# A new written-out succession for a fused RWKV and MLP-mixer kernel, with other conditions for its first weights

## The chip, the cores and the metric

The kernel runs on one core of one Trainium2 chip. The metric is the device time of one execution in microseconds; of several executions the median counts. The engines are PE (TensorE), DVE (VectorE), ACT (ScalarE), POOL (GpSimd) and SP (SyncE, which here only issues transfers). Each engine works off its own list of instructions strictly in order and waits at the head of the list for semaphores.

## The reference

Inputs are r, k, v of shape (4, 8, 768, 48), per-head vectors w and u, and four weight matrices. First a linear attention with decay runs over 768 steps of time for each batch and head; then the heads are put side by side into x of shape (4, 768, 384), and one mixer block follows:

```python
for t in range(S):
    cur = einsum('bhd,bhe->bhde', u * k[t], v[t])
    y[t] = einsum('bhd,bhde->bhe', r[t], state + cur)
    state = w * state + einsum('bhd,bhe->bhde', k[t], v[t])

h  = maximum(x.T @ w_tok1, 0) @ w_tok2        # over the 768 steps of time, inner width 256
u  = x + h.T
h2 = maximum(u @ w_ch1, 0) @ w_ch2            # over the 384 channels, inner width 1536
return u + h2
```

## The kernel before

**Tiling.** The 768 steps of one batch are cut into 6 chunks of 128, which makes 24 units (batch, chunk), all heads of a unit at once. A unit's k, r and v are three loads of 128 x 384 f32 (192 KB each) into pools of 8 buffers per kind.

**Attention of a unit u** is a fixed set of named steps: `kp`, `rp` scale k and r by powers of the decay (DVE or POOL), `trk`, `trr` transpose them on the PE (units 14 to 23 by a DMA transpose `i:t` instead), `rk` (or `rkk` and `rkr`) bring the result to SBUF (ACT), `at` makes the scores on the PE, `AT0`, `AT1` mask them (DVE, some after a copy `raw` on ACT), `vb` casts v (ACT), `kv` and `S` carry the state, `pr`, `pg`, `adg`, `yd` make the diagonal term, `yS` and `y` sum the output in PSUM, and `x` writes the unit's part of x. `yi` of unit 3 adds the diagonal term on the PE by an f32 matmul.

**Mixer of a batch.** `hid` multiplies the six chunks of x by w_tok1 (into `h1_ps`), `hr` is the relu, `bk` and `us` (or `ux` and `ub` for half of batch 0) make u, `tu` and `uT` turn it, `z` multiplies by w_ch1, `zr` is the relu, `h` multiplies by w_ch2, `os` adds, `i:o` stores. There are 24 `z` steps of three matmuls each in a batch, and 24 `h` steps of twelve matmuls in four parts.

**Weights.** They come by six transfers that POOL issues (`i:w0` w_tok1, `i:w1` w_tok2, `i:w2` and `i:w4` the halves of w_ch1, `i:w3` and `i:w5` the halves of w_ch2); these cast f32 to bf16. `hid` needs w0, `ub` and `bk` need w1, `z` needs w2 and later w4, `h` needs w3 and later w5. POOL works them off between its products.

**What sets the order.** `ORDER` (line 508) names for each engine the succession of its steps. A planner (`Plan.run`, line 70) replays these lists with assumed costs, from the settings in `CFG` (line 444); the sequence of start times that comes out of it is the sequence in which the steps are emitted. Its assumed times set three things in the program beside that: how many filler matmuls (`Plan.fill`, line 142) stand in gaps of the PE, which shared product of POOL or DVE waits for which (`products_in_turn`, line 158), and the turn in which pooled buffers are handed out. The engine's own order is that of `ORDER`.

In `CFG`, `wafter` gives for each weight a step that the planner lets its request wait for (`x:r4` is the landing of unit 4's r); it enters `graph` alone (line 426), and `weight` (line 753) issues a DMA with no condition beyond its place on POOL. `slack` lengthens the assumed landing of a load, `half` is the time up to which the planner takes the PE to be slow, and `y_m` lists the units whose output `y` has a PSUM bank of its own from the common pool of four in place of the fixed bank.

One condition is made in the program too: `hold` (line 495) keeps the load of a unit's k back until a step is done. `hold={6: ('y', 5), ...}` holds `i:k6` until the last matmul of `y5`, and with it everything behind `i:k6` on SP:

```python
if i in CFG.get("hold", {}) and nm == "k":
    first = INS["".join(map(str, CFG["hold"][i]))]
    tc.add_manual_dep(ins.ins, first.ins.name, ..., reason="weights first")
```

SP issues loads, stores and DMA transposes. The program has eight semaphores for them in turn, so a transfer is issued only when the eighth before it has landed.

PSUM has four banks in a common pool (`psM`) and four with fixed use (`psA`).

Of the kernel before, what the change touches and what calls it, by code (L numbers as in the profile page):

```python
# [180 lines left out]
def graph(do, cfg):  # L181
# [256 lines left out]
    for s in p.steps:  # L438
# [42 lines left out]
    wafter={0: 'x:r4', 1: 'kp5', 2: 'rp5', 4: 'rp5', 3: 'rp5', 5: 'rp5'},  # L481
    slack={'v5': 0.9},
# [16 lines left out]
    y_m=(2, 4),  # L499
    apart=2.0,  # L500
    half=8.3,
# [28 lines left out]
    ),  # L530
    "DVE": (
# [11 lines left out]
    ),  # L543
    "ACT": (
# [558 lines left out]
```

## Time and profile before

| | |
|---|---|
| median of 3 runs | 166.47 us (165.52 to 167.43) |
| the profiled execution, its own time | 165.6 us |
| its span, first to last instruction | 163.9 us |
| mean granted TensorE clock | 0.984 |
| PE busy | 154.8 us |
| DVE, ACT, POOL busy | 119.7, 74.0, 59.1 us |
| read from and written to HBM | 20.65 and 4.72 MB |

All durations below are of the one profiled execution. It was faster than the median of the runs by 0.9 us. A row of the timeline has the start in us, the length in us, the engine, the line, the operation and what it writes and reads; since a helper records every instruction, all have the line L617, and rows are told apart by engine and tile. "SPq" is the issue of a transfer by SP. A row of the windows has the stretch, its length, and for each engine the busy time with the count of instructions; then the granted clock of the PE, the busy share of the DMA engines and GB/s.

### The profile page before, as it was taken

How to read it: one execution, taken by the hardware profiler on the slowest of the kernel's cores; microseconds unless marked ns; L12 is line 12 of the kernel's file. 1: busy time of each engine (PE TensorE's matmuls, PEld its weight loads, DVE VectorE, ACT ScalarE, POOL GpSimd, SP SyncE). 2: the span in 40 equal slices, each digit the busy share in tenths (PEclk: the TensorE clock that was granted, in tenths of full speed). 3: DMA queues.
4: the chain of work that ended last, by engine and by line, in shares of the span. 5: the costliest groups of instructions: out<-in, count | busy, mean ns of one | idle time of the engine just before them, and what ended most of it. 6: DMA issues, size and time to landing. Idle time of an engine off the chain costs nothing.

```text
span 163.9 us, 3809 instructions
## 1 busy us (share of the span) xinstructions
PE 154.8 (94%) x1487; PEld 99.2 (61%) x1487; DVE 119.7 (73%) x254; ACT 74.0 (45%) x160; POOL 59.1 (36%) x74
## 2 busy tenths in 40 slices
PE   6988799999999999999999999999999999999990
PEld 3476565656576767665666565666566666655670
DVE  5679878547089998896998989999999665223330
ACT  4899671552389635588504420445134102621400
POOL 7157860000055495954459542182702000000000
PEclk9999789999999999999999999999999999999997
DMA  5999999999999998999499999999934032501212
GB/s 106 222 212 219 152 201 201 185 184 198 199 221 237 210 233 168 214 159 208 99 167 206 226 212 150 236 234 151 204 67 145 0 72 43 177 0 48 96 48 98
DMA packets 97427, 26.26 MB, mean 160 GB/s; under 512 B 90753, under 2 KB 97410, under 8 KB 97410
## 3 DMA queue, kind: packets, MB, share of 16 engines
q1 hardware_dynamic: 93920, 22.88, 69.9%
q0 software_dynamic: 3488, 3.15, 12.1%
q8 instruction: 11, 0.18, 0.4%
q14 instruction: 6, 0.05, 0.1%
q10 hardware_dynamic: 2, 0.00, 0.0%
HBM read 20.65 MB, written 4.72 MB: 155 GB/s over the span
## 4 chain that ended last, share of the span: by engine, by line
PE 84%; SPq 7%; DMA 3%; ACT 3%; issue 1%; DVE 0%; ACTq 0%
PE h_ps L617 34%; PE z_ps L617 29%; SPq L617 7%; PE y_ps L617 6%; PE at_ps L617 5%; PE hT_ps L617 4%; DMA ld_v<-in_v_dram 3%; PE tr_ps L617 3%; PE kv_ps L617 3%; ACT rk L617 1%; PE t_ps L617 1%; ACT raw L617 0%; ACT vb L617 0%; PE ut_ps L617 0%; ACT S L617 0%
## 5 line engine op out<-in xcount | busy, mean ns | idle before, releaser
L617 PE MATMUL h_ps<-wch,zr 128*128 128x384 bf16 (+1 forms) x300 | 55.2, 320 | 0.0
L617 PE MATMUL z_ps<-uT,wch 128*128 128x384 bf16 x288 | 53.9, 326 | 0.1
L617 ACT ACTIVATE zr<-z_ps 128x384 bf16<-128x384 f32 x66 | 30.8, 492 | 50.7 <-PE z_ps L617 50.2
L617 PEld LDWEIGHTS <-zr 128*128 128x128 bf16 x300 | 27.4, 98 | 15.2
L617 PEld LDWEIGHTS <-wch 128*128 128x128 bf16 x288 | 26.6, 98 | 16.2 <-issue 0.2
L617 DVE TENSOR_TENSOR AT<-at_ps,mask 128x512 bf16<-128x512 f32 x43 | 28.9, 684 | 1.5 <-PE at_ps L617 1.2
L617 DVE TENSOR_SCALAR zr<-z_ps 128x384 bf16<-128x384 f32 x30 | 15.9, 553 | 11.7 <-PE z_ps L617 11.2
L617 POOL TENSOR_TENSOR kpr<-ld_r,wp 128x384 bf16<-128x384 f32 x14 | 14.6, 1044 | 24.9 <-DVE pr L617 22.2
L617 POOL TENSOR_TENSOR kpr<-ld_k,wn 128x384 bf16<-128x384 f32 x16 | 16.3, 1019 | 10.0 <-DMA ld_k<-in_k_dram 5.8
L617 DVE TENSOR_TENSOR osb<-u_sb,h_ps 128x384 f32<-128x384 bf16 (+1 forms) x22 | 11.7, 532 | 11.0 <-PE h_ps L617 11.0
L617 ACT COPY rk<-tr_ps 128x512 bf16<-128x512 bf16 (+1 forms) x23 | 15.1, 682 | 8.9 <-PE tr_ps L617 8.8
L617 PEld LDWEIGHTS <-rk 48*128 48x128 bf16 (+1 forms) x272 | 11.0, 97 | 8.7 <-issue 4.6
L617 PEld LDWEIGHTS <-kpr 128*128 128x128 bf16 x192 | 12.5, 101 | 5.2 <-issue 1.6
L617 POOL TENSOR_TENSOR yd<-vb,adg 128x384 f32<-128x384 bf16 x12 | 10.3, 858 | 12.0 <-ACT vb L617 8.3
L617 DVE TENSOR_TENSOR x_b<-y_ps,yd 128x384 bf16<-128x384 f32 x23 | 12.6, 552 | 2.1 <-PE y_ps L617 1.9
L617 ACT CAST vb<-ld_v 128x384 bf16<-128x384 f32 x24 | 12.2, 514 | 3.4 <-DMA ld_v<-in_v_dram 3.3
L617 DVE TENSOR_TENSOR u_sb<-x_b,hT_ps 128x384 bf16<-128x384 bf16 x21 | 11.2, 549 | 2.3 <-PE hT_ps L617 1.9
L617 PE MATMUL tr_ps<-ident,kpr 128*128 128x128 bf16 x112 | 10.7, 233 | 1.0 <-ACT rk L617 0.6
L617 PEld LDWEIGHTS <-wtok 128*128 128x128 bf16 x90 | 8.1, 97 | 4.8 <-issue 0.4
L617 PE MATMUL at_ps<-rk 48*128 48x128 bf16 x192 | 9.8, 222 | 1.2 <-ACT rk L617 0.4
L617 DVE TENSOR_TENSOR pr<-tr_ps,rk 128x512 bf16<-128x512 bf16 x14 | 5.9, 419 | 5.9 <-ACT rk L617 5.8
L617 PE MATMUL h_ps<-x_b,wtok 128*128 128x384 bf16 x48 | 10.0, 325 | 0.0
(87 smaller groups left out, 157.5 us busy)
## 6 DMA issues: line engine op xcount, KB each, us to landing
ld_k<-in_k_dram SPq DMA_DIRECT2D x24, 192.0 KB, 3.8
ld_r<-in_r_dram SPq DMA_DIRECT2D x24, 192.0 KB, 3.9
ld_v<-in_v_dram SPq DMA_DIRECT2D x24, 192.0 KB, 3.8
out_dram<-osb SPq DMA_DIRECT2D x23, 192.0 KB, 2.3
wch<-in_moe_w_ch_dram POOLq DMA_DIRECT2D x4, 576.0 KB, 12.2
wtok<-in_moe_w_tok_dram POOLq DMA_DIRECT2D x2, 384.0 KB, 5.4
u_bc<-in_u_dram SPq DMA_DIRECT2D x1, 192.0 KB, 4.4
out_dram<-osb SPq DMA_DIRECT2D x2, 96.0 KB, 2.6
```

Source lines behind the costliest of these rows:

```text
L617: ins = tc.keep_in_program_order(f(*args, **kw))
```

## The change

Four settings of the planner are changed, and the succession of all five engines is written anew. The first weight's request waits in the plan for the landing of v of unit 4 in place of r of unit 4, the second and third for the landing of r of unit 5 in place of the products `kp5` and `rp5`. The assumed extra time of v5 goes from 0.9 to 0.6, the slow time of the PE from 8.3 to 9.0, and the units with an output bank of their own are 1, 3 and 5 in place of 2 and 4. `hold` stays as it was.

Only the heads of the lists are shown, up to about the first channel matmul of batch 0; behind that the steps of a list are the same but stand in another order, and some 60 steps go from one engine to another (21 `zr` from ACT to DVE and 19 the other way, some of `kp`, `rp`, `yd`, `ku`, `rku` between DVE and POOL).

```diff
-    wafter={0: 'x:r4', 1: 'kp5', 2: 'rp5', 4: 'rp5', 3: 'rp5', 5: 'rp5'},
-    slack={'v5': 0.9},
+    wafter={0: 'x:v4', 1: 'x:r5', 2: 'x:r5', 4: 'rp5', 3: 'rp5', 5: 'rp5'},
+    slack={'v5': 0.6},
...
-    y_m=(2, 4),
+    y_m=(1, 3, 5),
     apart=2.0,
-    half=8.3,
+    half=9.0,
...
     "PE": (
-        "trk0 trr0 trk1 at0 wu trr1 trk2 trr2 pg0 at1 y0 kv0 pg1 at2 pg2 kv1 trk3 trr3 yS1 yS2 y1 kv2 trk4 at3 pg3 trr4 kv3 y2 trk5 at4 yS3 "
-        "trr5 yi3 y3 kv4 pg4 at5 yS5 pg5 ux0_0_1 yS4 hid0_bank0 y4 y5 hid0_bank1 hid0_0 hid0_1 hid0_2 hid0_3 hid0_4 hid0_5 ux0_0_2 ux0_0_0 "
-        "ub0_0_0 bk0_3 ub0_0_2 bk0_5 ub0_0_1 bk0_4 tu0_3 tu0_5 z0_0_0 z0_0_4 tu0_4 z0_0_3 z0_0_2 z0_0_5 z0_1_0 z0_0_1 z0_0_9 z0_1_1 z0_1_2 "
+        "trk0 trr0 wu kv0 at0 trk1 pg0 trr1 trk2 trk3 y0 trr2 at1 yS1 kv1 pg1 trr3 at2 pg2 yS2 kv2 y1 trk4 y2 trr4 at3 trk5 pg3 kv3 yS3 at4 "
+        "trr5 yi3 y3 at5 yS4 pg5 y4 pg4 hid0_bank0 hid0_bank1 kv4 hid0_0 hid0_1 hid0_2 yS5 y5 hid0_3 ux0_0_2 hid0_4 hid0_5 ux0_0_0 ux0_0_1 "
+        "ub0_0_0 bk0_4 bk0_3 ub0_0_2 ub0_0_1 bk0_5 tu0_3 tu0_4 z0_0_0 tu0_5 z0_0_3 z0_0_4 z0_1_0 z0_1_1 z0_1_2 z0_0_1 z0_0_5 z0_0_2 z0_0_7 "
...
     "DVE": (
-        "kp1 kp0 rp0 rp2 rp1 pr0 AT0_0 uw AT1_0 pr1 yd0 AT0_1 x0 pr2 AT1_1 AT1_2 yd1 AT0_2 x1 pr3 AT0_3 S2 yd2 AT1_3 pr4 yd3 AT1_4 AT0_4 x2 "
-        "pr5 AT0_5 AT1_5 yd5 yd4 x4 x5 hr0_0a hr0_1b uT0_0_0 us0_3 us0_5 us0_4 uT0_5 uT0_3 zr0_0_3 zr0_0_9 zr0_0_4 zr0_0_11 zr0_1_1 "
+        "kp0 rp0 kp2 uw pr0 AT0_0 rp1 AT1_0 rp2 yd0 rp3 x0 pr1 AT0_1 yd1 pr2 AT0_2 AT1_1 AT1_2 S2 x1 yd2 pr3 AT1_3 AT0_3 x2 yd3 AT0_4 AT1_4 "
+        "pr4 pr5 AT0_5 AT1_5 yd4 yd5 x4 x5 hr0_0a hr0_1b us0_4 us0_3 uT0_0_0 us0_5 uT0_5 zr0_0_4 zr0_1_0 zr0_0_3 zr0_1_2 zr0_0_5 zr0_1_3 "
...
     "ACT": (
-        "lnw wn0 wn1 wp0 wp2 wn2 wp1 rkk0 rkr0 vb0 raw0 rkk1 rkr1 rkk2 rkr2 raw1 vb1 S0 vb2 S1 rk3 wGm vb3 rk4 S3 vb4 rk5 x3 S4 raw5 vb5 "
+        "lnw wn0 wn2 wp0 wp1 vb0 wn1 rkk0 rkr0 wp2 S0 raw0 rkk1 rkr1 vb1 rkk2 raw1 rkr2 wGm S1 vb2 rk3 rk4 vb3 vb4 rk5 S3 x3 raw5 vb5 S4 "
...
     "POOL": (
-        "kp2 kp3 rp3 kp4 rp4 i:w0 kp5 rp5 i:w1 i:w2 i:w4 i:w3 i:w5 rp8 kp8 kp9 kp10 yd7 yd8 rp11 yd9 rp12 kp12 yd10 yd11 rp13 kp13 yd12 "
+        "kp1 kp3 kp4 rp4 i:w0 kp5 rp5 i:w1 i:w2 i:w4 i:w3 i:w5 kp7 rp9 rp7 kp8 yd6 kp9 rp10 kp11 yd8 rp11 yd10 rp12 rp13 yd11 kp13 yd12 "
...
     "SP": (
-        "i:k1 i:r2 i:k0 i:r0 i:r1 i:v0 i:k2 i:v1 i:k3 i:r3 i:v2 i:k4 i:r4 i:k5 i:v3 i:r5 i:v4 i:v5 i:k6 i:r6 i:k7 i:r7 i:v6 i:r8 i:k8 i:v7 "
+        "i:k0 i:r0 i:v0 i:k2 i:k1 i:r1 i:k3 i:v1 i:r2 i:r3 i:v2 i:k4 i:v4 i:r4 i:k5 i:v3 i:r5 i:v5 i:k7 i:k6 i:r6 i:v6 i:r9 i:r7 i:r8 i:k8 "
...
```

More of the change, by code (lines that the diff above doesn't have):

```diff
@@ L509 @@
     "PE": (
[20 rows of a table removed]
[20 rows of a table added]
     ),
     "DVE": (
[11 rows of a table removed]
[11 rows of a table added]
     ),
     "ACT": (
[8 rows of a table removed]
[8 rows of a table added]
     ),
     "POOL": (
-        "kp2 kp3 rp3 kp4 rp4 i:w0 kp5 rp5 i:w1 i:w2 i:w4 i:w3 i:w5 rp8 kp8 kp9 kp10 yd7 yd8 rp11 yd9 rp12 kp12 yd10 yd11 rp13 kp13 yd12 "
-        "kp14 rp14 rp16 ku14 ku15 ku16 kp16 yd14 rku16 yd16 ku18 rku18 yd15 kp19 rp18 kp18 rp19 yd17 rku19 kp20 rp21 rku20 rp22 kp21 yd19 "
-        "kp23 ku23 rku22 rp23 yd23 "
[3 rows of a table added]
     ),
     "SP": (
[5 rows of a table removed]
[5 rows of a table added]
         "i:o3_3 i:o3_4 i:o3_5a i:o3_5b "
```

76 rows, old and new, of the table ORDER are left out of this document.

## The prediction

> **What bounds the kernel now.** I read the page's shares and its chain first, then the windows by stage, then the rows of the stage that the change moves.
>
> ```profile
> span 163.9 us, 3809 instructions
> PE 154.8 (94%) x1487; PEld 99.2 (61%) x1487; DVE 119.7 (73%) x254; ACT 74.0 (45%) x160; POOL 59.1 (36%) x74
> PE 84%; SPq 7%; DMA 3%; ACT 3%; issue 1%; DVE 0%; ACTq 0%
> ```
>
> TensorE (PE) is busy 94% of the span and holds 84% of the chain that ended last; the other shares of the chain lie at its start. The windows cut the span at the first matmul of the token mixing of batch 0 (24.64) and at the first matmul of its channel mixing (29.88); the last rows are shorter stretches.
>
> ```profile
> core 0: us, PE busy (x) PEld busy (x) DVE busy (x) ACT busy (x) POOL busy (x), PEclk, DMA share, GB/s
> 0.00:24.64 24.64, 20.23 (x253) 13.87 (x254) 18.41 (x50) 19.04 (x39) 15.70 (x29) 0.93 1.02 185
> 24.64:29.88 5.24, 5.19 (x44) 3.12 (x40) 4.38 (x10) 1.51 (x4) 0.00 (x0) 1.00 1.15 199
> 29.88:160.30 130.42, 129.40 (x1197) 82.19 (x1196) 96.90 (x196) 53.42 (x117) 43.45 (x45) 1.00 0.79 156
> 10.00:15.00 5.00, 4.31 (x89) 3.63 (x87) 4.73 (x14) 4.87 (x13) 3.35 (x5) 1.00 1.08 207
> 15.00:20.00 5.00, 3.67 (x65) 2.52 (x62) 4.43 (x10) 3.83 (x9) 4.43 (x5) 0.87 1.01 167
> 18.69:22.10 3.41, 3.29 (x32) 2.10 (x29) 2.98 (x6) 2.32 (x5) 3.41 (x5) 0.50 1.31 197
> 65.00:70.00 5.00, 4.60 (x58) 3.10 (x57) 4.57 (x11) 2.57 (x6) 5.00 (x7) 1.00 0.99 199
> ```
>
> From 29.88 on the PE is idle 130.42 - 129.40 = 1.02 us in all. The work behind that point is the same in both kernels (the two successions hold the same steps behind `z0_0_0`, but that `tu0_5` takes the place of `tu0_4`), so no succession can win more than 1.0 us there. The rest of what can be won lies ahead of 29.88: 24.64 - 20.23 = 4.4 us of idle PE, and a stretch of 3.41 us at half clock (0.50).
>
> What lets the first channel matmul go are two things: units 0 to 5 must be through attention, and the first part of `wch1` must have landed. The weights are asked for by POOL between its products:
>
> ```profile
> 14.90 1.00 POOL L617 TENSOR_TENSOR kpr<-ld_r,wp 128x384 bf16<-128x384 f32 x1
> 15.85 0.89 POOL L617 DMA_DIRECT2D wtok<-in_moe_w_tok_dram  x1
> 16.76 1.01 POOL L617 TENSOR_TENSOR kpr<-ld_k,wn 128x384 bf16<-128x384 f32 x1
> 18.32 0.99 POOL L617 TENSOR_TENSOR kpr<-ld_r,wp 128x384 bf16<-128x384 f32 x1 [0.55 <-DMA ld_r<-in_r_dram]
> 19.25 0.77 POOL L617 DMA_DIRECT2D wtok<-in_moe_w_tok_dram  x1
> 20.02 3.19 POOL L617 DMA_DIRECT2D wch<-in_moe_w_ch_dram  x4
> DMA to landing us min/median/max: 8.3/12.2/17.0
> ```
>
> The last line is from the view of the tile `wch`: the earliest of its four transfers took 8.3 us, so `w2` landed at about 20.02 + 8.3 = 28.3, 1.6 us before its first reader at 29.88. The six weights keep the DMA engines full from about 18 us to the last landing: the last of the four issues began near 20.02 + 3.19 - 0.8 = 22.4, and 22.4 + 17.0 = 39.4.
>
> **The change part by part.** *The weights' conditions (`wafter`).* They enter only the planner's graph; `weight()` issues a bare DMA. In POOL's written-out order `i:w0` stands behind `rp4` and `i:w1` behind `rp5` in both kernels, so in the program nothing is asked for earlier: the issue still hangs on r4 and r5. These edits cost and win nothing by themselves. The same holds for `slack` and `half`, beyond the filler matmuls (27 before, 28 now, 14 of them now in one place, behind `pg0`); they lie in gaps, so nothing for them.
>
> *The loads' order.* r4 goes from place 13 to 14 of SP's list, r5 from 16 to 17, v4 comes four places earlier. A load of 192 KB at the 207 GB/s of the 10 to 15 us row takes 0.95 us. So `rp4` moves from 14.90 to 15.85 at the latest, `w0` from 15.85 to 16.8, and `rp5`, which waited for its load until 18.32, to 19.3; `w1` and `w2` are asked for behind it, at 20.2 and 21.0.
>
> *A load slips past the hold.* SP was held at `i:k6` until the last matmul of `y5` (`hold={6: ...}`), which kept all later loads behind the weights' requests:
>
> ```profile
> 14.67 2.78 SPq L617 DMA_DIRECT2D ld_v<-in_v_dram  x2
> 24.83 0.37 SPq L617 DMA_DIRECT2D ld_k<-in_k_dram  x1
> 25.24 0.60 SPq L617 DMA_DIRECT2D ld_r<-in_r_dram  x1
> ```
>
> Now `i:k7` stands ahead of `i:k6`, and the hold is on k6 alone; k7 takes the eighth buffer and waits for nothing but old landings. Its 192 KB follow v5 at once, into the time when the weights move. What that costs can be read where both queues were busy (30 to 36 us, the second pair) and where the weights were alone (22 to 28 us, the first line), in the views of the DMA queues:
>
> ```profile
> q0 software_dynamic: 782, 1.15, 112.9%
> ...
> q0 software_dynamic: 1161, 0.89, 93.7%
> q1 hardware_dynamic: 1161, 0.22, 33.5%
> ```
>
> Alone the weights (q0) moved 1.15 MB in 6 us, 0.192 MB/us; beside loads (q1) 0.89 MB, 0.148 MB/us, while the loads got 0.037 MB/us, packet for packet the same count. k7's 0.197 MB beside weights would take 5.3 us and cost them 5.3 x 0.044 / 0.192 = 1.2 us. The other end is nothing: between 15 and 20 us the engines moved 167 GB/s against 207, a hole of 0.2 MB, as large as k7. I take 1.2, since the load comes last on SP, behind the hole. The Trainium skill, "DMA: Bandwidth & Descriptors", section "Queues, rings and completion order", has each engine take turns between queue rows packet by packet; the equal counts of 1161 agree, and the sum would be the same by it. The later requests of `w0` to `w2` cost little beside that, because the queue in front of them is then emptier by the same loads. So `w2` lands at 28.3 + 1.2 = 29.5 (28.3 to 30.4 with both in full).
>
> *Attention of unit 5.* Its chain ends in these rows, all at or just behind the half clock:
>
> ```profile
> 19.86 0.63 PE L617 MATMUL tr_ps<-ident,kpr 128*128 128x128 bf16 x4
> 20.28 1.59 PE L617 MATMUL y_ps<-yd,ident_w 128*128 128x384 f32 x2
> 22.02 0.37 PE L617 MATMUL kv_ps<-vb,kpr 128*128 128x96 bf16 x4
> 22.22 0.24 PE L617 MATMUL g_ps<-UW,pr 128*128 128x2 bf16 x4
> 22.39 0.40 PE L617 MATMUL at_ps<-rk 48*128 48x128 bf16 x8
> ...
> 22.61 0.64 ACT L617 CAST S<-kv_ps 48x192 bf16<-48x192 f32 x2
> 23.27 0.58 ACT L617 CAST raw<-at_ps 128x512 bf16<-128x512 f32 x1
> ...
> 23.88 0.43 DVE L617 TENSOR_TENSOR AT<-raw,mask_b 128x512 bf16<-128x512 bf16 x1 [0.36 <-ACT raw L617]
> 24.30 1.02 DVE L617 TENSOR_TENSOR yd<-vb,g_ps 128x384 f32<-128x384 bf16 x2
> 25.42 1.02 DVE L617 TENSOR_TENSOR x_b<-y_ps,yd 128x384 bf16<-128x384 f32 x2
> ...
> 29.88 1.14 PE L617 MATMUL z_ps<-uT,wch 128*128 128x384 bf16 x6
> ```
>
> `rp5` ended at 19.3 and its transpose began at 19.86, 0.55 us of slack; one slot later (0.95) leaves 0.4 us of delay for `trr5` and `yi3`. Behind `y3` the new succession has `at5` at once, with `kv4` and `pg4` behind it: they started 0.37 us ahead of it (22.02 to 22.39), so `at5` stays at about 22.4. ACT then does `raw5` ahead of `S4` (0.64), which lets it start at about 22.9, right behind `at5`, not at 23.27; DVE's masking follows at 23.5 for 23.88, and from there the list is the same length: two `yd`, two `x`. Three of the six token steps run before `y5` now; DVE's two `x` still gate the last two, so they hide no more. The attention thus lets the channel mixing go 0.0 to 0.4 us earlier, I take 0.2: 29.7. It ends last, `w2` (29.5) just before it. Term one: 29.7 - 29.88 = **-0.2 us**, from -1.3 (k7 in the hole, r5 on time) to +0.6 (`w2` at 30.4).
>
> *The rest of the succession.* From 29.88 some 60 steps change engines, about as many from DVE to ACT or POOL as back, and nearly all change place. No trace shows the new waits. The lower bound is all idle gone, -1.0. For the upper bound, in the list of waits of this stretch stands
>
> ```profile
> PE tr_ps L617 <- ACT rk L617: 0.6, 2, 0.4
> ```
>
> a mean of 0.3 us; the worst 5 us (65 to 70) have 0.40 idle. If ten of the 18 later units got such a wait, it would be +3.0. I take a doubling of today's idle, **+1.0 us**, nearest to the row of 1.02: each engine works strictly in its list, and a list fitted to assumed landings meets others.
>
> The sum against the profiled execution's own 165.6 (span 163.9 and 1.7 around it): 165.6 - 0.2 + 1.0 = 166.4. The median of the runs, 166.47, is 0.9 above that execution, so the forecast for a median is **167.3 us**.
>
> **The rivals.** *The weights come on time and the attention earlier* (faster): k7 fills the 0.2 MB hole, r5 is not late, and the channel mixing starts at 28.4, right behind `w2`: -1.5; half of the 1.0 idle goes: -0.5; 164.5 on the median. For it speaks the hole; against it that r5 stands a place later.
>
> *The late list* (slower): POOL and DVE lists of units 6 to 9 meet landings in another order than assumed, because k7 is there early and the weights, then k6 and r6, late. POOL has `rp9` ahead of `rp7` and `kp8`, at 1.0 us each, and `trk8` waits for `kp8`; a single late load holds the products behind it and, over the transposes, the PE. It decides once the loads behind the weights come over 0.5 us later than now; price ten waits of 0.3 us instead of the one us taken: +2.0, 169.3. Against it: today's list had to meet late landings too.
>
> *The half clock falls on full work* (slower). The stretch 18.69 to 22.10 follows a thin window (3.67 busy of 5.00). The new list has a thin place too, `trk5` waiting for `kp5`. Should the stretch come after 24.64, 1.7 us of matmul work is lost where no idle hides it: 169.0. Conversely the Trainium skill, "TensorE: Matmul & The Clock Gate", section "Why this matters for your kernels", says that only idle gaps of about 3 us throw the clock back. Such a kernel would have no half-clock stretch: the attention would be up to 1.7 us earlier, but `w2` at 29.5 holds the first channel matmul, so 167.1. The trace speaks against that rule: the 0.50 came with no PE gap that long, the whole idle of 15 to 20 us being 1.33.
>
> *It does nothing of what it says*: requests unmoved, the orders worth the same, 166.5.
>
> **How the numbers follow.** Chances: forecast 0.38, on-time 0.20, late list 0.20, half clock on full work 0.12, nothing 0.06, no half clock 0.04. One per cent of 166.47 is 1.7 us, about what a measurement of this kernel can tell from no change (three runs spread from 165.5 to 167.4). Faster (under 164.8) holds nearly all of the on-time case, 0.19; slower (over 168.1) the late list, nearly all of the half clock, and 0.05 of the forecast's spread, 0.35; within 1%: 0.46. The range, 164.4 to 169.6, reaches from the on-time case to just beyond the late list; what is left out is a half-clock stretch and a late list together, or all idle gone.
>
> **What would show it.** Right: k7's load issued right behind v5, before 20 us; `wch`'s shortest transfer longer than 8.3 us or asked for near 21; first `z_ps` between 29.4 and 30.2; PE idle behind it about 2 us. Wrong: a first `z_ps` before 29.0, PE idle over 3 or under 0.5 us behind it, or a row of clock under 1.00 after 24.64. If the r5 slot is not late at all, the load term has failed.

## The result

The changed kernel is slower: 167.86 us, the median of 4 executions (167.62 to 168.1), against 166.0 of the kernel before, measured beside it (4 executions, 165.03 to 167.43; the three of the first table are among them). These medians differ by 1.1%; the recorded ratio, which isn't simply that of the medians, is 1.0147, with a 95% interval from 1.0101 to 1.0193. The range that was forecast holds the time, and 167.3 lies 0.6 us below it. The class that had been given most (within 1%) holds the time against the 166.47 us that it was reckoned from, but not the ratio.

The ratios leave out executions that lie over 1.5% above the fastest of their kernel; of the kernel before these are 10 of 25, 4 of 13 and 16 of 34 on the three chips of the experiments, and with them its medians there would be 166.04, 166.59 and 166.49 in place of 165.75, 166.07 and 165.83, so that a ratio near 1.006 is hardly a difference.

The profiled execution took 167.8 us. From the page of the changed kernel, the span, the shares of the engines and the shares of the chain that ended last:

```profile
span 165.7 us, 3812 instructions
PE 156.0 (94%) x1488; PEld 100.5 (61%) x1488; DVE 119.7 (72%) x249; ACT 73.1 (44%) x160; POOL 64.4 (39%) x79
PE 76%; DVE 8%; SPq 7%; DMA 3%; POOL 2%; ACT 2%; issue 1%; POOLq 0%; DVEq 0%
```

The PE's share of the chain fell from 84% to 76%, and DVE and POOL came into it with 8% and 2%. Ahead of the first channel matmul lie 2.6 us of POOL's links and 3.4 of DVE's, where the kernel before has none of either; another 9 us of DVE's lie behind it. To see which of the two parts is longer I cut both spans at the first channel matmul and at the end of the last matmul. First the windows of the kernel before (columns as in the prediction), then those of the changed one:

```profile
15.00:16.00 1.00, 0.88 (x26) 0.71 (x22) 1.00 (x3) 0.91 (x3) 1.00 (x2) 1.00 1.16 232
16.00:17.00 1.00, 0.67 (x16) 0.33 (x8) 1.00 (x3) 0.64 (x2) 0.98 (x2) 1.00 0.64 121
29.88:159.92 130.04, 129.40 (x1197) 82.19 (x1196) 96.56 (x195) 53.42 (x117) 43.45 (x45) 1.00 0.79 156
159.92:163.90 3.98, 0.00 (x0) 0.00 (x0) 0.35 (x1) 0.00 (x0) 0.00 (x0) 0.77 0.30 98
```

```profile
15.00:16.00 1.00, 0.68 (x10) 0.48 (x11) 1.00 (x4) 0.95 (x3) 0.10 (x1) 1.00 0.40 74
17.43:24.26 6.83, 5.77 (x56) 3.88 (x58) 5.27 (x11) 3.49 (x7) 6.62 (x9) 0.50 1.18 188
31.34:162.35 131.01, 130.02 (x1197) 83.07 (x1197) 95.33 (x189) 52.38 (x117) 48.60 (x50) 1.00 0.78 154
162.35:165.70 3.35, 0.00 (x0) 0.00 (x0) 0.35 (x1) 0.00 (x0) 0.00 (x0) 1.00 0.27 87
```

The first channel matmul comes at 31.34 in place of 29.88 (+1.46), the stretch from it to the last matmul takes 131.01 in place of 130.04 (+0.97), and what follows the last matmul 3.35 in place of 3.98 (-0.63). Together +1.80, the difference of the spans. Around the span lie 2.1 us in place of 1.7.

How the start became late is read from the chain that ended last. Some of its links between 12 and 20 us, first of the kernel before, then of the changed one (start, length, what):

```profile
12.83 4.69 DMA ld_v<-in_v_dram
```

```profile
12.29 4.37 DMA ld_r<-in_r_dram
...
17.66 0.90 POOL wtok L617
18.58 1.02 POOL kpr L617
```

Before, the chain ran over the landing of v3; now it runs over the landing of r4 and from there along POOL. POOL's timeline in the changed kernel:

```profile
16.72 1.00 POOL L617 TENSOR_TENSOR kpr<-ld_r,wp 128x384 bf16<-128x384 f32 x1 [1.62 <-DMA ld_r<-in_r_dram]
17.66 0.90 POOL L617 DMA_DIRECT2D wtok<-in_moe_w_tok_dram  x1
18.58 1.01 POOL L617 TENSOR_TENSOR kpr<-ld_k,wn 128x384 bf16<-128x384 f32 x1
19.78 1.00 POOL L617 TENSOR_TENSOR kpr<-ld_r,wp 128x384 bf16<-128x384 f32 x1 [0.19 <-DMA ld_r<-in_r_dram]
...
21.49 3.19 POOL L617 DMA_DIRECT2D wch<-in_moe_w_ch_dram  x4
24.67 1.04 POOL L617 TENSOR_TENSOR kpr<-ld_k,wn 128x384 bf16<-128x384 f32 x1
```

`rp4` begins at 16.72 in place of 14.90 and waited 1.62 us for its load. Behind it on POOL follow at once the request of w0 (0.90 us of POOL's own time) and `kp5`, whose own load k5 had landed at 17.40: it was the queue that held it until 18.58. `rp5` is 1.46 us later than before for two reasons that nearly coincide: the queue was done with `kp5` at 19.59, and r5 itself landed late, so that `rp5` waited 0.19 us more for it.

r4 was late mainly because it was asked for late. Its issue on SP, before and in the changed kernel:

```profile
10.76 1.23 SPq L617 DMA_DIRECT2D ld_r<-in_r_dram  x1
```

```profile
12.29 0.81 SPq L617 DMA_DIRECT2D ld_r<-in_r_dram  x1
```

Of these 1.53 us, 0.52 had arisen by the issue of k4 (10.51 in place of 9.99; the loads of units 0 to 3 stand in another order too), and 0.99 is the issue of v4, which now stands between k4 and r4. The transfer itself took 4.4 us in place of 4.0. The hole at 15 to 16 us, in which the DMA engines moved 74 GB/s where the kernel before had 232 in the same microsecond, falls on it and can have cost this difference.

The PE takes this up twice, and the half clock falls on what follows (PE timeline of the changed kernel):

```profile
17.77 0.61 PE L617 MATMUL tr_ps<-ident,kpr 128*128 128x128 bf16 x4 [0.63 <-POOL kpr L617]
...
19.64 0.61 PE L617 MATMUL tr_ps<-ident,kpr 128*128 128x128 bf16 x4 [0.72 <-POOL kpr L617]
...
21.79 0.61 PE L617 MATMUL tr_ps<-ident,kpr 128*128 128x128 bf16 x4
...
24.14 0.43 PE L617 MATMUL at_ps<-rk 48*128 48x128 bf16 x8
...
31.34 0.65 PE L617 MATMUL z_ps<-uT,wch 128*128 128x384 bf16 x3
```

`trr4` waited 0.63 us for `rp4`, with `at3` behind it in the list, and `trk5` 0.72 us for `kp5`. `trr5` then began at 21.79, 1.01 us after the end of `rp5` (20.78): by then it was the PE, at half clock from 17.43 to 24.26 and without a gap from 19.64 on, that was late. `at5` came at 24.14 in place of 22.39, and the first channel matmul 1.46 late.

Two more lines of the changed kernel, the issue of k7 on SP and the landings of the tile `wch`:

```profile
17.61 0.91 SPq L617 DMA_DIRECT2D ld_k<-in_k_dram  x1
```

```profile
DMA to landing us min/median/max: 8.3/12.0/16.9
```

k7 slipped past SP's hold, as forecast, and `w2` landed at 21.49 + 8.3 = 29.8, 1.5 us before its reader: the weights did not hold the first channel matmul.

### The profile page after: what moved, and what is told of

It is laid out like the page before. It is cut to its first block, busy times and chain, and to the rows that moved or that the text cites. A ratio compares the mean times of both kernels' runs of the same rounds, so it can differ in the third digit from the quotient of the medians.

```text
span 165.7 us, 3812 instructions
## 1 busy us (share of the span) xinstructions
PE 156.0 (94%) x1488; PEld 100.5 (61%) x1488; DVE 119.7 (72%) x249; ACT 73.1 (44%) x160; POOL 64.4 (39%) x79
## 4 chain that ended last, share of the span: by engine, by line
PE 76%; DVE 8%; SPq 7%; DMA 3%; POOL 2%; ACT 2%; issue 1%; POOLq 0%; DVEq 0%
PE h_ps L617 30%; PE z_ps L617 27%; SPq L617 7%; PE hT_ps L617 4%; PE y_ps L617 4%; PE at_ps L617 4%; DMA ld_r<-in_r_dram 3%; PE kv_ps L617 2%; DVE AT L617 2%; PE tr_ps L617 2%; DVE x_b L617 2%; DVE yd L617 1%; POOL kpr L617 1%; ACT rk L617 1%; DVE S L617 1%
## 5 line engine op out<-in xcount | busy, mean ns | idle before, releaser
L617 PE MATMUL h_ps<-wch,zr 128*128 128x384 bf16 (+1 forms) x300 | 54.4, 320 | 0.0
L617 ACT ACTIVATE zr<-z_ps 128x384 bf16<-128x384 f32 x64 | 29.3, 490 | 54.0 <-PE z_ps L617 53.9
L617 PE MATMUL z_ps<-uT,wch 128*128 128x384 bf16 x288 | 52.8, 326 | 0.0
L617 DVE TENSOR_SCALAR zr<-z_ps 128x384 bf16<-128x384 f32 x32 | 16.9, 553 | 11.8 <-PE z_ps L617 10.8
L617 POOL TENSOR_TENSOR kpr<-ld_r,wp 128x384 bf16<-128x384 f32 x15 | 15.4, 1033 | 25.0 <-DMA ld_r<-in_r_dram 20.3
L617 POOL TENSOR_TENSOR kpr<-ld_k,wn 128x384 bf16<-128x384 f32 x15 | 15.5, 1034 | 12.3 <-DMA ld_k<-in_k_dram 8.3
L617 POOL TENSOR_TENSOR yd<-vb,adg 128x384 f32<-128x384 bf16 x13 | 11.1, 853 | 22.3 <-DVE adg L617 17.3
L617 DVE TENSOR_TENSOR u_sb<-x_b,hT_ps 128x384 bf16<-128x384 bf16 x21 | 10.7, 549 | 5.4 <-PE hT_ps L617 5.4
L617 PE MATMUL h_ps<-x_b,wtok 128*128 128x384 bf16 x48 | 10.5, 326 | 0.1
L617 PE MATMUL hT_ps<-h1r,wtok 128*128 128x384 bf16 x42 | 9.3, 326 | 0.2 <-ACT h1r L617 0.2
```

Of the source, the lines that this page charges most:

```text
L617: ins = tc.keep_in_program_order(f(*args, **kw))
```

## The experiments

Every kernel was measured beside the kernel before, on the same chip. The medians are of the executions that the ratio of each uses; the other columns are from the one profiled execution, "rest" being the stretch from the first channel matmul (first z) to the end of the last matmul.

| kernel | median (n) | ratio and interval | rp5 | first z | rest | behind it |
|---|---|---|---|---|---|---|
| before | 165.75, 166.07, 165.83 (15, 9, 18) | 1 | 18.32 | 29.88 | 130.04 | 3.98 |
| after | 167.86 (4) | 1.0147 [1.0101, 1.0193] | 19.78 | 31.34 | 131.01 | 3.35 |
| x1 | 167.62 (3) | 1.0107 [1.0041, 1.0172] | 18.40 | 30.11 | 132.01 | 3.38 |
| x2 | 167.65 (9) | 1.0116 [1.0074, 1.0157] | 19.84 | 31.79 | 130.83 | 3.58 |
| x3 | 166.83 (7) | 1.0059 [1.0004, 1.0114] | 18.42 | 32.02 | 130.69 | 3.79 |
| x7 | 165.48 (9) | 0.9999 [0.9952, 1.0046] | 19.13 | 31.07 | 130.82 | 4.01 |
| x4 | 168.61 (4) | 1.0151 [1.0089, 1.0212] | 20.31 | 32.03 | 132.02 | 3.35 |
| x5 | 168.1 (4) | 1.0117 [1.0061, 1.0173] | 20.13 | 31.75 | 131.31 | 3.34 |
| x6 | 166.57 (9) | 1.0039 [0.9992, 1.0086] | 19.02 | 30.16 | 131.00 | 3.34 |
| x9 | 167.9 (4) | 1.0110 [1.0054, 1.0166] | 20.00 | 31.57 | 131.01 | 3.32 |
| y1 | 167.66 (9) | 1.0083 [1.0051, 1.0116] | 19.69 | 31.25 | 130.99 | 3.36 |
| y2 | 166.92 (9) | 1.0062 [1.0022, 1.0102] | 18.16 | 30.76 | 131.99 | 3.35 |
| y3 | 166.97 (11) | 1.0067 [1.0024, 1.0110] | 19.19 | 30.15 | 131.03 | 3.92 |
| y4 | 167.32 (10) | 1.0114 [1.0068, 1.0159] | 18.59 | 30.16 | 130.99 | 3.35 |

The profiled executions of x3, x7 and y2 were 1.2 to 2.1 us above their medians and that of x4 0.8, while that of y4 was 0.8 below, so their first z is not typical.

### The start and the rest, each alone (x1, x2)

x1 has the start of the kernel before (units 0 to 5, loads, weights, token mixing of batch 0) and the changed succession behind it; the settings and the heads of the other three lists go back as well. Against the changed kernel, on POOL and SP:

```diff
-        "kp1 kp3 kp4 rp4 i:w0 kp5 rp5 i:w1 i:w2 i:w4 i:w3 i:w5 kp7 rp9 rp7 kp8 ...
+        "kp2 kp3 rp3 kp4 rp4 i:w0 kp5 rp5 i:w1 i:w2 i:w4 i:w3 i:w5 kp7 rp9 rp7 kp8 ...
-        "i:k0 i:r0 ... i:k4 i:v4 i:r4 i:k5 i:v3 i:r5 i:v5 i:k7 i:k6 i:r6 ...
+        "i:k1 i:r2 ... i:k4 i:r4 i:k5 i:v3 i:r5 i:v4 i:v5 i:k6 i:k7 i:r6 ...
```

> The start of the kernel before (all steps of units 0 to 5, the loads and weights, the token mixing of batch 0) with the succession of the changed kernel behind it; k7's load stands behind the held k6. In the changed kernel the first channel matmul came 1.46 us later than before and the stretch from there to the last matmul was 0.97 us longer (131.06 against 130.09). If these two are separate: first z_ps at 29.9 within 0.4, stretch 131.0, time 0.6 to 1.0 above the kernel before. Rival, that the longer stretch only echoes the late start (loads and weights coming late into units 6 to 9): stretch 130.1, time as before within 0.3.

Measured: 1.0107, with the first channel matmul as early as before (30.11) but a rest of 132.01. The windows, the PE's waits behind 30 us and the timeline of POOL, all of x1:

```profile
30.11:162.12 132.01, 130.16 (x1200) 83.18 (x1197) 94.97 (x188) 52.43 (x116) 49.99 (x51) 1.00 0.77 154
```

```profile
PE tr_ps L617 <- ACT rk L617: 0.7, 1, 0.7
PE tr_ps L617 <- POOL kpr L617: 0.3, 1, 0.3
PE kv_ps L617 <- DVE S L617: 0.3, 1, 0.3
PE t_ps L617 <- DVE u_sb L617: 0.3, 1, 0.3
```

```profile
39.82 0.99 POOL L617 TENSOR_TENSOR kpr<-ld_k,wn 128x384 bf16<-128x384 f32 x1 [16.52 <-DMA ld_k<-in_k_dram]
```

The last line is `kp7`, the first product behind the weights in the changed POOL list, with `rp9`, `rp7` and `kp8` queued behind it. With k7 behind the held k6 it ran at 39.82; in the changed kernel, where k7 slips past, it ran at 24.67. So x1 does not hold the rest as the changed kernel has it. The table sorts by this: the changed succession with k7 early takes 130.99 to 131.01 behind the first channel matmul in five kernels, and 131.31 in x5; with k7 held 131.99 to 132.02 in three (x1, x4, y2). The early k7 is worth 1.0 us there. And the same 131.0 stands in x6 with an early first z (30.16) as in the changed kernel with a late one: a rest that is only an echo of the late start is ruled out.

x2 is the other half: the changed start, k7 ahead of k6 included, and the succession of before behind it (in the two lists of the diff above, the changed line up to `i:w5` and up to `i:k6`, and then the steps of before).

> The start of the changed kernel (with k7's load ahead of the hold) and the succession of the kernel before behind it. Separate parts: first z_ps at 31.3 within 0.4, stretch 130.1, time 1.0 to 1.6 above the kernel before. Rival, echo: stretch 131 again, time as the changed kernel, 1.8 above.

Measured: 1.0116; first z 31.79. The start alone costs nearly all that the change costs. The parts add to 2.2%, more than the 1.5% of both; x1's part also pays for the held k7, 1.0 us or 0.6%.

### The conditions and the fillers (x3, x7)

x3 is the kernel before with the new conditions only:

```diff
-    wafter={0: 'x:r4', 1: 'kp5', 2: 'rp5', 4: 'rp5', 3: 'rp5', 5: 'rp5'},
+    wafter={0: 'x:v4', 1: 'x:r5', 2: 'x:r5', 4: 'rp5', 3: 'rp5', 5: 'rp5'},
```

> The kernel before with the new conditions of the weights in the planner alone: every engine's succession is the old one, the only change in the program is that the planner sees other gaps and puts in 50 filler matmuls for 27. Conditions do nothing: w0 asked for at 15.9 as before, time within 0.4 of before. Clock theory (the half clock comes from a thinly used PE and costs time): with 23 more fillers the half-clock stretch is shorter or gone and the first z_ps up to 1 us earlier, time up to 1 us less.

Measured: 1.0059, and the requests stay where they were (w0 at 16.14, before at 15.85). The conditions ask for nothing earlier. They move the planner's times, and with them the fillers: 50 where the kernel before has 27.

x7 is the kernel before without fillers:

```diff
-    fill=(0.2, 0.08, 0.107),
```

> The kernel before without any filler matmul. Clock theory: the PE is thinner between 7 and 17 us, the half clock lasts 6.8 us as in the changed kernel or longer, first z_ps 1.0 to 1.5 later, time 1 to 1.5 above before. Chain theory (the start is paced by the loads, POOL's products and DVE, and the PE has slack there): clock down likewise, but first z_ps within 0.5 and time within 0.5 of before.

Measured: 0.9999. The 27 fillers of the kernel before are worth nothing that can be measured, nor do they cost anything. Whether the 23 more of x3 are its 0.6% isn't shown: its interval begins at 1.0004. They bring no gain, in any case, as the clock theory had it for x3; nor did x7 lose what that theory had for it.

### k7 held back (x4)

```diff
-        "... i:r5 i:v5 i:k7 i:k6 i:r6 ...
+        "... i:r5 i:v5 i:k6 i:k7 i:r6 ...
```

> The changed kernel with k7's load moved behind the held k6 on SP. The prediction's price of the early k7: the weights 1.2 us earlier, w2 at 28.6 for 29.8 and w5 at 39.4 for 40.7. Since the first z_ps of the changed kernel stood at 31.34, 1.5 us behind w2, attention ends last there: first z_ps and time unchanged within 0.4. Rival, that the late weights carry the loss: time 1.0 to 1.3 less.

Measured: 1.0151, no gain. In the profiled execution the weights came later, not earlier: the first channel matmul waited for `w2`. PE timeline, tile `wch` and windows of x4:

```profile
32.03 0.66 PE L617 MATMUL z_ps<-uT,wch 128*128 128x384 bf16 x3 [0.45 <-DMA wch<-in_moe_w_ch_dram]
```

```profile
DMA to landing us min/median/max: 10.0/14.2/19.1
```

```profile
32.03:164.05 132.02, 130.17 (x1197) 83.19 (x1197) 94.90 (x188) 52.25 (x116) 49.98 (x51) 1.00 0.78 155
```

The shortest transfer of `wch` took 10.0 us where the changed kernel, with k7 beside it, has 8.3. Over all the profiled executions it took 7.3 to 9.7 us in the seven kernels with k7 early and 7.5 to 10.0 in the seven with k7 held. That k7 costs the weights 1.2 us is not borne out; why they were slower in x4 is not shown. Holding k7 costs the rest its 1.0 us.

### w0 asked for behind kp5 (x5)

```diff
-        "... kp4 rp4 i:w0 kp5 rp5 i:w1 ...
+        "... kp4 rp4 kp5 i:w0 rp5 i:w1 ...
```

> The changed kernel with POOL's request for w0 (0.90 us) moved behind kp5. Chain theory: rp4, request, kp5, trk5 stand in one row on POOL and PE, so kp5 starts at 17.7 for 18.58, trk5 0.9 earlier, and as rp5 waits for its load anyway (19.64), first z_ps 0.3 to 0.6 earlier, time 0.2 to 0.6 less; w0 lands near 25.1. If the late w0 holds the token mixing instead: its first matmul at 25.9 for 25.48 and no gain. Clock theory: no change.

Measured: 1.0117 on the chip where x9 has 1.0110. `kp5` came right behind `rp4` at 18.28, but r4 was late here too (`rp4` at 17.33), and `w0` was asked for at 19.21. `w0` landed at 25.7 and `w2` at 31.5, shortly ahead of their first readers (26.27 and 31.75), so that with an earlier `kp5` the first channel matmul could have come at most 0.2 us earlier here. In this execution the clock was at half for 10.24 us (windows of x5):

```profile
15.23:25.47 10.24, 9.27 (x108) 6.62 (x105) 7.89 (x16) 6.13 (x12) 8.12 (x10) 0.50 0.97 154
```

So the request ahead of `kp5` can't be had back for nothing: behind `kp5` it brings w0 and w2 nearly to their readers.

### v4 behind r5 again (x6)

```diff
-        "... i:k4 i:v4 i:r4 i:k5 i:v3 i:r5 i:v5 i:k7 ...
+        "... i:k4 i:r4 i:k5 i:v3 i:r5 i:v4 i:v5 i:k7 ...
```

> The changed kernel with v of unit 4 loaded behind r5 again, so that r4, k5, v3 and r5 are each one place earlier. Chain theory: rp4 starts 0.9 earlier (15.8 for 16.72), with it the request for w0, kp5 and rp5; first z_ps 0.7 to 1.0 earlier, near 30.5, time 0.6 to 1.0 less. Rival, that the half clock of 6.8 us makes the late start: the stretch stays and first z_ps moves by less than 0.3.

Measured: 1.0039 with an interval that holds 1. By the recorded ratios this one load takes back 1.1 points of the 1.5 (by the medians, on two chips, 0.8 of 1.1). POOL's timeline (`rp4`, `rp5`), the PE's and a window of x6:

```profile
16.20 1.01 POOL L617 TENSOR_TENSOR kpr<-ld_r,wp 128x384 bf16<-128x384 f32 x1 [1.01 <-DMA ld_r<-in_r_dram]
...
19.02 1.01 POOL L617 TENSOR_TENSOR kpr<-ld_r,wp 128x384 bf16<-128x384 f32 x1
```

```profile
24.68 1.15 PE L617 MATMUL h_ps<-x_b,wtok 128*128 128x384 bf16 x6 [1.33 <-DMA wtok<-in_moe_w_tok_dram]
...
30.16 0.65 PE L617 MATMUL z_ps<-uT,wch 128*128 128x384 bf16 x3
```

```profile
20.00:25.00 5.00, 3.45 (x61) 2.42 (x59) 4.65 (x11) 3.42 (x8) 3.90 (x6) 1.00 1.22 189
```

`rp5` is 0.76 us earlier than in the changed kernel, the clock is full, and the first token matmul now waits 1.33 us for `w0`; the first channel matmul comes 1.18 earlier. `rp4` is only 0.52 earlier, with a wait of 1.01 for r4: here a hole in the loads (81 GB/s at 16 to 17 us) fell on r4 too. The chain still runs over r4, now by way of the request of w0 behind `rp4`, which landed at 24.63. Since the clock is full in x6 as well, its gain isn't that of the load alone.

### at3 ahead of trr4 (x9)

```diff
-        "... trk4 y2 trr4 at3 trk5 pg3 ...
+        "... trk4 y2 at3 trr4 trk5 pg3 ...
```

> The changed kernel with at3 ahead of trr4 on the PE. at3's input (rk3) ended at 17.17, but trr4 ahead of it waited for rp4 until 17.72, so at3 came at 18.32. If that order is part of the loss: at3 at 17.3, the maskings of unit 3, x2 and yd3 0.7 to 1.0 earlier, first z_ps up to 0.5 earlier. If the load of r5 and rp5 (20.78) set the end alone: at3 earlier, first z_ps unchanged within 0.2.

Measured: 1.0110, first z 31.57. PE timeline of x9:

```profile
18.13 0.40 PE L617 MATMUL tr_ps<-ident,kpr 128*128 128x128 bf16 x4 [0.71 <-POOL kpr L617]
...
19.99 0.40 PE L617 MATMUL tr_ps<-ident,kpr 128*128 128x128 bf16 x4 [1.47 <-POOL kpr L617]
```

`at3` came at 17.02 in place of 18.32, and the first channel matmul no earlier. The wait at `trr4` stays (0.71), and that at `trk5` is 1.47 in place of 0.72: what is no longer queued behind the one is idle ahead of the other. This piece of the PE's order is not the cause; the PE waits for POOL's queue, and POOL for r4.

### More fillers, for the clock (y1)

Thirty fillers more, behind six steps of the start, so that the PE has no thin stretch there:

```diff
+    more={"kv1": 6, "trr3": 2, "at2": 4, "pg2": 3, "y2": 7, "at3": 8},
```

> The changed kernel with 30 more filler matmuls on the PE in the places where it waited between 13 and 19.6 us (behind kv1, trr3, at2, pg2, y2 and at3); loads, POOL, DVE and ACT as in the changed kernel. Clock theory: the PE is no longer thin, the half clock of 6.8 us is gone or shorter, the PE's full row from 19.6 to 24.6 shrinks by up to 2 us, first z_ps at 30.0 to 30.5 (w2 landed at 29.83), time 0.7 to 1.2 less. Chain theory (r4, rp4, request for w0, kp5, trk5, rp5 set the start whatever the clock): first z_ps unchanged within 0.4, time unchanged.

Measured: 1.0083, and 167.66 against 167.86 of the changed kernel, on other chips. The clock was full in this execution (1.00 in the first line below), and `at5` came at 22.82, 1.3 us earlier than in the changed kernel; the first channel matmul came at 31.25, only 0.09 earlier. Windows, PE, DVE and POOL timeline of y1:

```profile
20.00:25.00 5.00, 4.77 (x79) 3.41 (x77) 4.76 (x10) 4.10 (x11) 4.99 (x7) 1.00 1.22 185
```

```profile
22.82 0.44 PE L618 MATMUL at_ps<-rk 48*128 48x128 bf16 x8
```

```profile
24.32 1.57 DVE L618 TENSOR_TENSOR AT<-raw,mask_b 128x512 bf16<-128x512 bf16 x1 [0.24 <-ACT raw L618]
```

```profile
24.58 1.02 POOL L618 TENSOR_TENSOR kpr<-ld_k,wn 128x384 bf16<-128x384 f32 x1
```

What the clock won was lost in `AT1_5`, which took 1.57 us in place of the 0.43 that it takes in the kernel before: it began 0.94 us earlier than in the changed kernel and ended 0.11 earlier, beside `kp7` of POOL. The chain of y1 doesn't run over r4 at all; it goes over DVE's maskings and the PE, and over `AT1_5`. In all nine executions of y1 the mean granted clock was 0.996 or more, in the four of the changed kernel between 0.967 and 0.990, and the medians differ by 0.2 us. So a full clock alone doesn't bring the loss back in this order. How much it would bring without the collision, these runs don't say. (The mean clock says nothing of the first microseconds, as the last section shows; in the profiled execution of y1 the matmuls are at full speed from about 9 us on.)

### Both remedies, and the best of the parts (y2, y3, y4)

y2 has v4 behind r5 and k7 behind k6 (the diffs of x6 and x4 together).

> The changed kernel with v4 behind r5 and k7's load behind the held k6. With v4 back alone, the first token-mixing matmul waited 1.33 us for w0 (landed 24.63, 7.5 after its request; 5.6 in the kernel before, which held k7). If k7 beside w0 is the reason: w0 lands 1 to 1.5 earlier, the wait is gone, first z_ps at 29.3 to 29.8 for 30.16, time 0.3 to 0.8 less than with v4 back alone (1.0039 of before), so at or just under the kernel before. Rival: w0 as late without k7, nothing gained.

Measured: 1.0062. Its rest is 131.99, the one of the held k7. w0 landed 8.6 us after its request with no k7 beside it, later than the 7.5 of x6, so holding k7 gains nothing at the start either.

y3 has y2's start and the succession of before behind it.

> The same start (v4 behind r5, k7 held), with the succession of the kernel before behind the start. If the parts add up: first z_ps at 29.3 to 29.8, stretch to the last matmul 130.1 to 130.8 for 131.0, last part 3.6 to 3.9 for 3.4; time as before within 0.5, at best 0.3 less. Rival: a start that is earlier than the lists assume makes the units 6 to 9 wait for loads, the stretch grows by what the start wins, and the time is 0.5 above before.

Measured: 1.0067. Even with the loads from k4 on in the old order, k7 held and the old rest, the new heads of the lists (the order of the loads of units 0 to 3 among them) are not better than those of before; no version here beats the kernel before.

y4 is x6 without any fillers (the `fill` line taken out, as in x7).

> The changed kernel with v4 behind r5, without any filler matmul. With fillers it ran at full clock from 6.9 us on. Clock theory: without them the PE is thin, a half-clock stretch returns within the first 25 us, first z_ps 0.7 to 1.5 later, time about as the changed kernel, 1.3 to 1.5 per cent above before. Chain theory: the clock may fall, but first z_ps stays within 0.4 of 30.16 and the time within 0.4 of v4 back alone.

Measured: 1.0114, by medians 0.7 us above x6, though the profiled execution, the fastest of its ten, came out like x6's (first z 30.16, rest 130.99). Fillers may help this start, which waits more; the intervals of x6 and y4 overlap, so it isn't shown.

## Why the prediction came out as it did

**Where the time is.** The gap of the medians is 1.86 us. In the pair of profiles the start holds 1.46. For the rest and what lies behind it, the five profiled executions with the succession of before (before, x2, x3, x7, y3) take 134.0 to 135.0 us, with a middle of 134.5; the six with the changed one and an early k7 (after, x5, x6, x9, y1, y4) 134.3 to 134.7. (The profiled executions of x3 and x7 were late by their start alone; their rest is like the others'.) So the rest, which had been given the one positive term of the sum, is not shown to be slower at all, and the start, which had been given -0.2, is nearly the whole loss.

**The conditions: right on the requests.** x3 shows them unmoved. That the conditions cost nothing by themselves isn't shown: x3 is 1.0059 with 50 fillers, the changed kernel has 28.

**The fillers: right where tried.** x7 prices those of before at 0.9999.

**The loads' order: the right mechanism, mis-sized.** One slot of 0.95 us was taken, and `rp4` came 1.82 later, `rp5` 1.46. The slot is there (0.99 us for the issue of v4). What was missed is that k4 ahead of it was asked for 0.52 late already, and that the list is not worked off at the even 207 GB/s of one row: a hole of a microsecond (74 GB/s) fell on r4, which took 0.4 us longer. Such a hole stands in the kernel before too, at 16 to 17 us (121 GB/s), but `rp4` had begun at 14.90. Its cause was not found. That v4's place matters stands in all the traces: `rp4` begins at 16.70 to 17.33 in the six kernels with the changed order of loads, at 14.90 to 15.29 in the four with that of before, and in the four with v4 back at 15.02, 15.29, 16.20 and 16.30, the last two behind a hole.

**k7: half right.** It slipped past at 17.61, as forecast, and `w2` landed at 29.8 (29.5 forecast), but for another reason: the request was 1.47 later and the transfer as long as before (8.3). The 1.2 us that k7 was to cost are not borne out, and what wasn't seen is that the changed POOL list needs it: `kp7` stands first behind the weights, and with k7 held the rest is 1.0 us longer.

**Attention of unit 5: the step that failed.** "0.55 us of slack; one slot later (0.95) leaves 0.4", and `at5` to stay at 22.4. `at5` came at 24.14, term one at +1.46 where -0.2 had been taken and +0.6 was its upper end. The working read the slack at `rp5` and its transpose, over which the chain runs in neither kernel. It left out that `rp4`, the request and `kp5` are one unbroken queue on POOL, so that r4's delay is that of all; that the PE meets this queue twice before `trr5` (0.63 and 0.72), and x9 shows that the wait only moves when one of the two is gone round; and that the half clock then lies on work without a gap. How the 1.75 us of `at5` divide is told by one pair of executions alone: y1, with `rp4` as late (16.70) and a full clock, has `at5` at 22.82, 0.43 behind the kernel before. There the half clock weighs more than the queue. The rival that put the half clock on full work had the mechanism, but behind 24.64, where the clock never fell; the clock took 6.83 us of the start instead. And no term stood for what the early `kp7` does to the masking of unit 5, 0.3 us in the changed kernel and 1.1 in y1.

**The rest: right in the pair, by luck.** +1.0 had been forecast and +0.97 is the difference of the two profiled stretches. But PE idle went only from 0.64 (130.04 - 129.40) to 0.99 (131.01 - 130.02), so the doubling that was the ground for it holds by half, and the other 0.62 us are busy time of the PE at the same 1197 matmuls, which nobody had forecast and which isn't explained here. (The 1.02 of idle that the prediction doubled held 0.38 us that lie behind the last matmul, at 159.92.) 0.63 comes back behind the last matmul; and 130.04 is the shortest of five executions with the same succession, the others 130.7 to 131.0.

**The sum.** +0.8 us on the profiled execution was forecast, +2.2 measured (165.6 to 167.8). That 167.3 lies near 167.86 owes something to the median before, 166.47 of three executions then and 166.0 of four now. The measured ratio of 1.0147 lies in the case "slower by over 1%", which had 0.35. Of the signs that were to show the forecast right, k7's issue before 20 us (17.61) and the request of `wch` near 21 (21.49) came true; the first channel matmul between 29.4 and 30.2 (31.34) and about 2 us of idle PE behind it (0.99) did not. None of the signs of being wrong showed, so they were too wide to catch this loss.

**The rivals.** The on-time case falls with r4, and the channel mixing at 28.4 with it. The late list falls: it was priced at +2.0 behind the first channel matmul, where these are all the waits of the PE in the changed kernel (list of waits from 31.34 on: total, times, longest):

```profile
PE kv_ps L617 <- DVE S L617: 0.5, 2, 0.3
PE hT_ps L617 <- ACT h1r L617: 0.2, 1, 0.2
```

Its mechanism is real all the same: with k7 held, as in x1, `kp7` comes late and the rest is 1.0 us longer. *No half clock* falls in this order: y1 had a full clock and a channel matmul only 0.09 earlier. *Nothing* falls with x2.

**Open.** How much of the loss belongs to the clock in a typical execution, since the order with a full clock lost the gain to a collision. x2, which has no `kp7` behind the weights, gives a hint: its three executions with a mean granted clock of 0.966 to 0.979 took 167.9 to 168.6 us, the six with 0.990 or more 166.3 to 167.7, and the middle of these six, 167.4, still lies 1.7 above 165.75. Open are also what makes the hole in the loads; and what in the heads of the lists of y3 makes its 0.67%, so far as that is a difference.

## What to carry to other kernels

Where products, transfer requests and more products stand in one strict queue, price a late load at the head of the queue, not at the step that ends last: everything behind the head inherits its delay, and slack read at the end of the queue isn't slack for the head. Read first over which landing the chain runs, before and after. A load that is pulled forward in an issue list pushes another back, so read first which of the two has an engine waiting at its landing. And when a written-out list takes a product early, find the transfer that it assumes: here the load past the hold looked like a cost and was what the list needed.

## What was not expected of the hardware

**A masking on DVE beside a product on POOL.** Five maskings of the form `AT<-raw,mask_b` are in every kernel (minimum, median and maximum in ns, view of the tile; the first fence is before, the second y4, in which the longest ran from 23.20 beside `kp7` of POOL):

```profile
L617 DVE TENSOR_TENSOR AT<-raw,mask_b x5: 414/416/427, 10.5 to 56.3; 128x512 bf16<-128x512 bf16 x5
```

```profile
L616 DVE TENSOR_TENSOR AT<-raw,mask_b x5: 405/414/1601, 10.7 to 57.4; 128x512 bf16<-128x512 bf16 x5
```

The kernel before had no POOL product near its masking of unit 5. The early k7 puts `kp7` right there: the masking takes 1.57 us in y1, 1.60 in y4, 1.09 in x9, 0.83 in x5, 0.74 in the changed kernel, and 0.43 in x6, where `kp7` came at 25.05, after the masking. In all five with an overlap it ends 0.29 us after `kp7`, whichever of the two began first. The Trainium skill, "SBUF — State Buffer", section "Who interferes with whom", says that a DVE instruction with both inputs in SBUF contends with a POOL instruction that reads SBUF, and that the one issued first has the port; the extra time of the two longest, 1.1 to 1.2 us, about one product of 1.02, agrees with the first. The second agrees in x9, x5 and the changed kernel, where `kp7` began first, but not in y1 and y4: there the masking began 0.26 and 0.28 us ahead of the product by the records and was the one that paid.

**Half a clock without a gap.** The half-clock stretches behind the first full one were 6.83 us in the changed kernel, 10.24 in x5 and 3.41 in x9 and y4. Two of them by the windows of x9 and y4:

```profile
20.61:24.02 3.41, 3.41 (x32) 2.16 (x29) 2.53 (x5) 1.53 (x3) 3.41 (x5) 0.50 1.27 171
```

```profile
11.43:14.84 3.41, 3.39 (x48) 2.53 (x45) 3.40 (x8) 3.04 (x8) 0.96 (x1) 0.50 1.09 216
```

The lengths are one, two and three times 3.41. The Trainium skill, "TensorE: Matmul & The Clock Gate", section "What's actually happening", has a free-running window of 3413 ns, and the lengths agree with it. Its rule that a whole idle window takes the clock back doesn't account for these stretches: from 5 us to the end of the stretch no gap of the PE was longer than 0.72 us in the changed kernel, 1.47 in x9 and 1.5 in y4.

**A clock of 1.00 that wasn't one.** The page of x7 prints a full clock from the start and the mean is 1.000. Yet its transposes take as long as those of the changed kernel at half clock (0.61 us for four), and not the 0.40 us of x9:

```profile
21.49 0.63 PE L616 MATMUL tr_ps<-ident,kpr 128*128 128x128 bf16 x4
```

From 23.29 on its matmuls are as short as elsewhere. In x3 four transposes take 0.63 us at 18.13 and 0.38 at 19.34. These two executions, 2.1 and 1.4 us above their medians, thus ran at half speed for the first 23 and 19 us, and the granted clock doesn't say so: what it prints ahead of its first change has to be compared with the lengths of the matmuls. The same holds for every mean clock above.
